# Pooled attention and two feed-forwards on one core: the softmax exponential head by head on ScalarE, straight from PSUM, with its sum from the same instruction

## The chip, the cores and the metric

The kernel runs on one core of a Trainium2 chip. The metric is device time in microseconds (us) of one execution. A core has TensorE (matrix products), VectorE, ScalarE and GpSimd, and SyncE, which here only issues transfers. The profile calls them PE, DVE, ACT, POOL and SP; each takes its instructions in order.

## What is computed

Attention over pooled keys and values, then a feed-forward with a squared relu, then a gated one:

```python
k_p = k.reshape(B, H, Sp, pool, D).mean(axis=3)      # 8 batches, 8 heads, 72 pooled keys, D = 64
v_p = v.reshape(B, H, Sp, pool, D).mean(axis=3)
scores = scale * np.matmul(q, k_p.transpose(0, 1, 3, 2))
scores = scores - np.max(scores, axis=-1, keepdims=True)
attn = np.exp(scores)
attn = attn / (np.sum(attn, axis=-1, keepdims=True) + 1e-09)
x = np.matmul(attn, v_p)                             # 4608 tokens of 512
h = np.maximum(x @ w_in, 0.0)
x = (s * (h * h) + b) @ w_out                        # 2048 wide
out = sigmoid(x @ w_gate) * (x @ w_val) @ w_out2     # 1536 wide
```

The feed-forward weights come as 64-bit words and are converted to float32 on the chip. Every product of the feed-forwards is made of three passes over a high and a low part of its operands.

## The kernel before

The 4608 tokens are cut into 18 **units** of 256 tokens, a unit into two **halves** of 128 (t = 0, 1), and the 8 heads into two groups of four (c = 0, 1). For a half, `scores` makes two score tiles in PSUM (`sps`, 128 tokens x 4 heads x 72 keys), takes the maximum over keys (`mx`), subtracts it into an SBUF tile `e` of 8 x 72 columns, and after the second group takes the exponential of all of `e` in one ScalarE instruction. `norm` sums `e` over keys (`sm`), scales and inverts the sum, and GpSimd multiplies: `pm` holds keys 0 to 63, `pl` the last 8. `left` splits `pl` into `lt`; `turn` transposes `pm` (`tm`) and `lt` (`tl`) on TensorE and splits the results; `values` makes the value product `pv`, whose split is the input `xh`, `xl` of the first feed-forward.

In PSUM the pool `ps_c` has two buffers. Score tiles (from unit 2 on), `tm`, `tl` and `pv` take them in turn: for a half both buffers go to its two score tiles, and the next two tiles of the pool wait until these have been read.

The first feed-forward runs in steps, 16 for each block of 512 tokens: `emit_h` (into `hps`), an evacuation and square on ScalarE and VectorE, a split into `gh` and `gl` (L55, L56), and two steps later `emit_x` (into `acc`). Its weights are converted during the first 16 steps, by ScalarE (L80, L55), VectorE (L81 to L83) and GpSimd (L56). The attention of unit u is strewn over these steps by a table of events: scores of half 0 at the beginning of a span of eight steps, of half 1 two steps later, `turn` of half 0 one step behind those, and so on. The weights of the second feed-forward are prepared beside steps 18 and on (`prep_w2`, again L80 to L83). The second feed-forward begins when all 144 steps are done and has no attention.

What sets the order on the engines: units 0 and 1 stand in an order written by hand. In the first 16 steps a scheduler orders all engines; from step 16 on TensorE's order is that of the code, and the scheduler orders the others. Pool buffers and data give the waits.

Of the kernel before, what the change touches and what calls it, by code (L numbers as in the profile page):

```python
# [8 lines left out]
F32 = mybir.dt.float32  # L9
F32R = mybir.dt.float32r  # L10
I32 = mybir.dt.int32
ACTF = mybir.ActivationFunctionType
ALU = mybir.AluOpType
AX = mybir.AxisListType
# [5 lines left out]
def pooled_attention_two_ffn(ctx, tc, q, k, v, v_left, w_in, w_out, s_in, b_in, w_gate, w_val, w_out2, out):  # L20
# [8 lines left out]
    nc = tc.nc  # L29
    NT, DM = out.shape  # L30
    NU, _, NP, UNIT = q.shape
    B, _, _, POOL, _, SP = k.shape
    S = SP * POOL
    D = 64
    H = 2 * NP
# [64 lines left out]
    at2 = at_stack.enter_context(tc.tile_pool(name="at2", bufs=2, side="right"))  # L100
# [235 lines left out]
    q_t, e_t, l_t, t_t = {}, {}, {}, {}  # L336

    def segs(t0, n):

        done = 0  # L340
        while done < n:
            b, s = divmod(t0 + done, S)
            step = min(n - done, S - s)
            yield done, step, b, s
            done += step
# [8 lines left out]
    s_t = {}  # L354

    def scores(u, t, c, pool=None):
        if c == 0:
            s_t[u, t] = (at2.tile([128, H, SP], F32, tag="e", name="e"), at2.tile([128, H], F32, tag="mx", name="mx"))
        e, mx = s_t[u, t]
        ps = (ps_a if pool else ps_c).tile([128, 4, SP], F32, tag="a" if pool else "c", name="sps")  # L360
        for i in range(2):
            for off, n, b, _ in segs(u * UNIT + t * 128, 128):
                nc.tensor.matmul(
                    out=ps[off:off + n, 2 * i:2 * i + 2, :].rearrange("p h j -> p (h j)"),
                    lhsT=q_t[u][:, 2 * i + c, t * 128 + off:t * 128 + off + n],
                    rhs=kbd[b % 2][:, 2 * i + c].rearrange("p two j -> p (two j)"),
                    start=True, stop=True,
                )
        h = slice(4 * c, 4 * c + 4)
        nc.vector.tensor_reduce(out=mx[:, h], in_=ps, axis=AX.X, op=ALU.max)  # L370
        nc.vector.tensor_tensor(out=e[:, h], in0=ps, in1=mx[:, h].unsqueeze(2).to_broadcast([128, 4, SP]),
                                op=ALU.subtract)
        if c == 1:
            nc.scalar.activation(out=e, in_=e, func=ACTF.Exp, scale=1.0 / (POOL * float(D) ** 0.5))
            if t == 1:
                q_t.pop(u)

    def norm(u, t, early=False):
        e, _ = s_t.pop((u, t))
        sm = at2.tile([128, H], F32, tag="sm", name="sm")  # L380
        nc.vector.tensor_reduce(out=sm, in_=e, axis=AX.X, op=ALU.add)
        nc.vector.tensor_scalar(out=sm, in0=sm, scalar1=float(POOL), scalar2=POOL * 1e-9, op0=ALU.mult, op1=ALU.add)
        nc.vector.reciprocal(out=sm, in_=sm)
        if early:
            pm = gp.tile([128, 512], F32, tag="g", name="pm", bufs=2).rearrange("p (h j) -> p h j", h=H)
        else:
            pm = at1.tile([128, H, 64], F32, tag="pm", name="pm")
        pl = at2.tile([128, H, 8], F32, tag="pl", name="pl")
        for o, j in ((pl, slice(64, SP)), (pm, slice(0, 64))):
            nc.gpsimd.tensor_tensor(out=o, in0=e[:, :, j], in1=sm.unsqueeze(2).to_broadcast(list(o.shape)), op=ALU.mult)  # L390
        e_t[u, t] = pm, pl
# [76 lines left out]
    for u in range(2, NU):  # L468
        p = 16 * (u - 2) + (2 if u == 2 else 0)
        for t, o in ((0, 0), (1, 4)):  # L470
            at(p + o, scores, u, t, 0)
            at(p + o, scores, u, t, 1)
            at(p + o + 2, norm, u, t)
            at(p + o + 3, left, u, t)
            if t == 0:
                at(p + 6, turn, u, 0, 0)
                at(p + 6, turn, u, 0, 1)
        at(p + 10, turn, u, 1, 0)
        at(p + 10, turn, u, 1, 1)
        at(p + 7, load_q, u + 2)  # L480
        at(p + 12, values, u, 0)
        at(p + 13, values, u, 1)

    def probs(u, t):
        scores(u, t, 0, True)
        scores(u, t, 1, True)
# [5 lines left out]
    with tc.manual_schedule():  # L492
# [22 lines left out]
        probs(0, 0)  # L515
        probs(0, 1)
        norm(0, 0, True)
        pool_v_pe(0, "v")
        left(0, 0)
        probs(1, 0)  # L520
        norm(0, 1, True)
        turns(0, 0)
        place_v(0)
# [16 lines left out]
    if True:  # L540
# [61 lines left out]
        for i in range(NS):  # L602
# [7 lines left out]
            x, r = divmod(i - 20, 8)  # L610
# [205 lines left out]
```

## Time and profile before

| | us |
|---|---|
| median of 3 runs | 1792.96 (1792.5 to 1793.54) |
| profiled execution | 1793.74 |
| its span | 1792.0 |
| busy: PE, DVE, ACT, POOL | 1739.8, 937.2, 774.8, 550.1 |

The span is from the first to the last instruction of the profiled execution; the 1.7 us around it are start and end. Busy times are sums over an engine's instructions. The mean granted clock of TensorE is 0.989 of full speed; only the first slices of the page show less than 9 tenths.

### The profile page before, as it was taken

To read this page: it belongs to the slowest core of one execution; us is meant where nothing else is said; L and a number is where in the kernel's file an instruction comes from. 1 tells how busy PE (TensorE), PEld (TensorE's weight loads), DVE (VectorE), ACT (ScalarE), POOL (GpSimd) and SP (SyncE) were. 2 spreads that over 40 slices of the span, in tenths; PEclk is the share of its full clock that TensorE was granted. 3 is DMA by queue.
4 is the path that set the end of the run, shared out by engine and by line. 5 is a ranking of instruction groups with operands and counts; after the bars stand their busy time and mean duration, and the time that the engine had idled before them with its cause. 6 is when DMAs were issued, how large, how long until landed. Compare 5 with 4: busy or idle time off the path is not lost.

```text
span 1792.0 us, 21860 instructions
## 1 busy us (share of the span) xinstructions
PE 1739.8 (97%) x8064; PEld 1446.9 (81%) x8064; DVE 937.2 (52%) x1491; ACT 774.8 (43%) x1390; POOL 550.1 (31%) x592
## 2 busy tenths in 40 slices
PE   5788999999999999999999999999999999999999
PEld 4667888888888888888887888888888888888887
DVE  6897747556465656444443545554545454545111
ACT  2566444444444545444444434343424343444122
POOL 3764504224042322010002443144314431443132
PEclk8989999999999999999999999999999999999999
DMA  6776735647383736332433334733473347333642
GB/s 229 261 227 211 273 123 198 223 165 250 112 267 123 265 118 223 118 118 94 141 106 144 118 109 146 251 114 113 144 253 110 117 141 256 106 118 115 235 140 83
DMA packets 84282, 298.18 MB, mean 166 GB/s; under 512 B 9808, under 2 KB 10832, under 8 KB 84176
## 3 DMA queue, kind: packets, MB, share of 16 engines
q1 hardware_dynamic: 80976, 286.30, 46.7%
q0 software_dynamic: 3200, 10.49, 1.7%
q8 instruction: 64, 1.05, 0.2%
q14 instruction: 42, 0.34, 0.1%
HBM read 250.61 MB, written 46.14 MB: 166 GB/s over the span
## 4 chain that ended last, share of the span: by engine, by line
PE 72%; issue 4%; DMA 1%; POOL 1%; DVE 0%; ACT 0%; POOLq 0%; DVEq 0%
PE pc L664 5%; PE pc L663 5%; PE pc L662 5%; PE acc L718 5%; PE acc L720 5%; PE acc L719 5%; PE pb L664 4%; PE pb L663 4%; PE pb L662 4%; PE hps L196 4%; PE hps L198 4%; PE hps L197 4%; PE acc L227 4%; PE acc L229 4%; PE acc L228 4%
## 5 line engine op out<-in xcount | busy, mean ns | idle before, releaser
L56 POOL TENSOR_TENSOR w<-w 128x512 fp32r<-128x512 f32 x264 | 254.4, 996 | 505.2 <-ACT w L55 481.7
L668 DVE TENSOR_TENSOR wk<-pc,wk 128x512 f32<-128x512 f32 x192 | 132.3, 689 | 240.8 <-PE pc L664 240.7
L196 PE MATMUL hps<-xl,wi 128*128 128x512 f32 (+1 forms) x584 | 234.5, 402 | 5.5 <-ACT g L200 2.6
L198 PE MATMUL hps<-xh,wi 128*128 128x512 f32 (+1 forms) x584 | 227.4, 389 | 0.0
L197 PE MATMUL hps<-xh,wi 128*128 128x512 f32 (+1 forms) x584 | 227.1, 389 | 0.0
L227 PE MATMUL acc<-gl,woh 128*128 128x512 f32 x576 | 225.5, 391 | 0.2 <-DVE gl L56 0.2
L228 PE MATMUL acc<-gh,woh 128*128 128x512 f32 x576 | 225.2, 391 | 0.0
L229 PE MATMUL acc<-gh,wol 128*128 128x512 f32 x576 | 225.0, 391 | 0.0
L56 DVE TENSOR_TENSOR gl<-g,gh 128x512 fp32r<-128x512 f32 x204 | 156.7, 768 | 129.6 <-ACT gh L55 124.6
L55 ACT ACTIVATE gh<-g 128x512 fp32r<-128x512 f32 x204 | 128.2, 628 | 142.5 <-DVE g L680 139.7
L204 DVE TENSOR_TENSOR g<-g 128x512 f32<-128x512 f32 x128 | 97.9, 765 | 150.3 <-ACT g L200 150.3
L205 ACT ACTIVATE g<-g,b_sb,s_sb 128x512 f32<-128x512 f32 x144 | 117.3, 814 | 126.4 <-DVE g L204 125.6
L662 PE MATMUL pc<-xo,w 128*128 128x512 f32 x432 | 168.1, 389 | 0.0
L664 PE MATMUL pc<-xo,w 128*128 128x512 f32 x432 | 168.1, 389 | 0.0
L663 PE MATMUL pc<-xo,w 128*128 128x512 f32 x432 | 168.0, 389 | 0.0
L200 ACT ACTIVATE g<-hps 128x512 f32<-128x512 f32 x144 | 85.3, 593 | 176.5 <-PE hps L198 174.6
L55 ACT ACTIVATE w<-w 128x512 fp32r<-128x512 f32 x264 | 113.3, 503 | 100.4 <-DMA w<-w7d 100.4
L664 PE MATMUL pb<-xo,w 128*128 128x512 f32 x336 | 131.6, 392 | 1.7 <-POOL w L56 1.7
L196 PEld LDWEIGHTS hps<-xl,wi 128*128 128x128 f32 x584 | 111.0, 190 | 26.8 <-ACT g L200 2.8
L662 PE MATMUL pb<-xo,w 128*128 128x512 f32 x336 | 131.3, 391 | 0.5 <-ACT w L55 0.5
L663 PE MATMUL pb<-xo,w 128*128 128x512 f32 x336 | 131.2, 390 | 0.0
L198 PEld LDWEIGHTS hps<-xh,wi 128*128 128x128 f32 x584 | 110.6, 189 | 23.5
(113 smaller groups left out, 3245.5 us busy)
## 6 DMA issues: line engine op xcount, KB each, us to landing
wi<-w1d SPq DMA_DIRECT2D x128, 512.0 KB, 3.4
wo<-wo2d SPq DMA_DIRECT2D x108, 512.0 KB, 3.5
w<-w7d SPq DMA_DIRECT2D x48, 896.0 KB, 4.4
raw<-in SPq DMA_DIRECT2D x68, 512.0 KB, 4.6
kv<-in SPq DMA_DIRECT2D x24, 512.0 KB, 5.2
kv<-in SPq DMA_DIRECT2D x16, 576.0 KB, 4.7
cv<-x2d POOLq DMA_DIRECT2D x36, 256.0 KB, 5.9
out<-eo SPq DMA_DIRECT2D x36, 256.0 KB, 4.2
```

The costliest lines, as they stand in the source:

```text
L55: nc.scalar.activation(out=hi, in_=src, func=ACTF.Copy)
L56: eng.tensor_tensor(out=lo, in0=src, in1=hi.bitcast(F32), op=ALU.subtract)
L196: nc.tensor.matmul(out=ps[:, f], lhsT=hi[:, kk], rhs=c[:, kk, f], start=kk == 0, stop=False)
L197: nc.tensor.matmul(out=ps[:, f], lhsT=hi[:, kk], rhs=a[:, kk, f], start=False, stop=False)
L198: nc.tensor.matmul(out=ps[:, f], lhsT=lo[:, kk], rhs=a[:, kk, f], start=False, stop=kk == KD - 1)
L227: nc.tensor.matmul(out=acc[j][d], lhsT=hi[:, f], rhs=gl, start=m == 0, stop=False)
L228: nc.tensor.matmul(out=acc[j][d], lhsT=hi[:, f], rhs=gh, start=False, stop=False)
L229: nc.tensor.matmul(out=acc[j][d], lhsT=lo[:, f], rhs=gh, start=False, stop=m == M1 - 1)
L662: nc.tensor.matmul(out=ps, lhsT=w[:, 0, x, kk], rhs=r[:, 1, kk, :n], start=first and kk == 0, stop=False, skip_group_check=True)
L663: nc.tensor.matmul(out=ps, lhsT=w[:, 0, x, kk], rhs=r[:, 0, kk, :n], start=False, stop=False, skip_group_check=True)
L664: nc.tensor.matmul(out=ps, lhsT=w[:, 1, x, kk], rhs=r[:, 0, kk, :n], start=False, stop=kk == 1, skip_group_check=True)
L668: nc.vector.tensor_tensor(out=o, in0=ps, in1=b_, op=ALU.add)
```

## The change

The subtraction on VectorE and the sum over keys on VectorE are taken out. VectorE now multiplies the maximum by minus the scale, and ScalarE takes the exponential of each head by itself, from PSUM, with that as its bias, and writes the head's sum over keys with the same instruction (`accum_out`).

```diff
     def scores(u, t, c, pool=None):
         if c == 0:
-            s_t[u, t] = (at2.tile([128, H, SP], F32, tag="e", name="e"), at2.tile([128, H], F32, tag="mx", name="mx"))
-        e, mx = s_t[u, t]
+            s_t[u, t] = (at2.tile([128, H, SP], F32, tag="e", name="e"), at2.tile([128, H], F32, tag="mx", name="mx"),
+                         at2.tile([128, H], F32, tag="sm", name="sm"))
+        e, mx, sm = s_t[u, t]
+        scale = 1.0 / (POOL * float(D) ** 0.5)
...
         nc.vector.tensor_reduce(out=mx[:, h], in_=ps, axis=AX.X, op=ALU.max)
-        nc.vector.tensor_tensor(out=e[:, h], in0=ps, in1=mx[:, h].unsqueeze(2).to_broadcast([128, 4, SP]),
-                                op=ALU.subtract)
-        if c == 1:
-            nc.scalar.activation(out=e, in_=e, func=ACTF.Exp, scale=1.0 / (POOL * float(D) ** 0.5))
-            if t == 1:
-                q_t.pop(u)
+        nc.vector.tensor_scalar(out=mx[:, h], in0=mx[:, h], scalar1=-scale, scalar2=None, op0=ALU.mult)
+        for i in range(4):
+            x = 4 * c + i
+            nc.scalar.activation(out=e[:, x], in_=ps[:, i], func=ACTF.Exp, scale=scale, bias=mx[:, x:x + 1], accum_out=sm[:, x:x + 1])
+        if c == 1 and t == 1:
+            q_t.pop(u)
 
     def norm(u, t, early=False):
-        e, _ = s_t.pop((u, t))
-        sm = at2.tile([128, H], F32, tag="sm", name="sm")
-        nc.vector.tensor_reduce(out=sm, in_=e, axis=AX.X, op=ALU.add)
+        e, _, sm = s_t.pop((u, t))
```

The order on ScalarE at the start of the program, with the engines that an instruction waits for behind it. Before (`e` is the exponential, `t` and `v1h` are splits of transposes and values):

```order
L374 ACT_TABLE_LOAD
L374 ACTIVATE e<-e 128x576 [waits DVE_49] x2
L398 ACTIVATE lt<-pl 128x16x8 [waits Pool_49]
L374 ACTIVATE e<-e 128x576 [waits DVE_49,Activation_49,Pool_49]
L55 ACTIVATE t_274<-tm 128x4x128 [waits PE_49]
```

and of the change:

```order
L376 ACT_TABLE_LOAD [waits DVE_49]
L376 ACTIVATE e,sm<-sps,mx 128x72 [waits PE_49]
L376 ACTIVATE e,sm<-sps,mx 128x72 x3
L376 ACTIVATE e,sm<-sps,mx 128x72 [waits DVE_49,PE_49]
L376 ACTIVATE e,sm<-sps,mx 128x72 x3
L376 ACTIVATE e,sm<-sps,mx 128x72 [waits DVE_49,PE_49]
L376 ACTIVATE e,sm<-sps,mx 128x72 x3
L376 ACTIVATE e,sm<-sps,mx 128x72 [waits DVE_49,PE_49]
L376 ACTIVATE e,sm<-sps,mx 128x72 x3
L398 ACTIVATE lt<-pl 128x16x8 [waits Pool_49]
```

Sixteen short instructions stand where two long ones stood, and the load of ScalarE's function table waits for VectorE, where it waited for nothing. Behind the `lt` of the first half come eight more in place of one, and then the split of `tm`.

On VectorE, in unit 1 (`raw` is a weight tile that is being converted), before:

```order
L370 TENSOR_REDUCE mx<-sps 128x4
L81 TENSOR_SCALAR raw<-raw 128x512
L371 TENSOR_TENSOR e<-sps,mx 128x288
L370 TENSOR_REDUCE mx<-sps 128x4
L371 TENSOR_TENSOR e<-sps,mx 128x288
L381 TENSOR_REDUCE sm<-e 128x8
```

and of the change:

```order
L372 TENSOR_REDUCE mx<-sps 128x4
L81 TENSOR_SCALAR raw<-raw 128x512
L373 TENSOR_SCALAR mx<-mx 128x4
L372 TENSOR_REDUCE mx<-sps 128x4
L373 TENSOR_SCALAR mx<-mx 128x4
L382 TENSOR_SCALAR sm<-sm 128x8
```

A multiply stands in the place of each subtraction, the sum over keys is gone, and L81 has kept its place between the maximum and what uses it.

On VectorE, at the second half of unit 9, where the scheduler sets the order, before:

```order
L399 TENSOR_TENSOR lt<-pl,lt 128x16x8
L56 TENSOR_TENSOR gl<-g,gh 128x512
L204 TENSOR_TENSOR g<-g 128x512
L56 TENSOR_TENSOR gl<-g,gh 128x512
L370 TENSOR_REDUCE mx<-sps 128x4 x2
L371 TENSOR_TENSOR e<-sps,mx 128x288 x2
L381 TENSOR_REDUCE sm<-e 128x8
```

and of the change:

```order
L56 TENSOR_TENSOR gl<-g,gh 128x512
L204 TENSOR_TENSOR g<-g 128x512
L56 TENSOR_TENSOR gl<-g,gh 128x512
L372 TENSOR_REDUCE mx<-sps 128x4 x2
L373 TENSOR_SCALAR mx<-mx 128x4 x2
L382 TENSOR_SCALAR sm<-sm 128x8
```

The two maxima stand behind the same splits as before; behind them two multiplies have taken the place of the two subtractions.

## Rows read from the trace of the kernel before

**Rows 1.** Busy us (instructions) by engine in two stretches, granted clock, DMA share, GB/s.

```profile
core 0: us, PE busy (x) PEld busy (x) DVE busy (x) ACT busy (x) POOL busy (x), PEclk, DMA share, GB/s
45.00:165.00 120.00, 98.59 (x478) 80.69 (x479) 110.97 (x157) 78.12 (x144) 78.70 (x62) 0.93 0.74 248
165.00:850.00 685.00, 682.41 (x3349) 573.14 (x3348) 386.68 (x654) 320.50 (x548) 179.89 (x197) 1.00 0.52 177
```

**Rows 2.** Groups by line and shape: count, busy us, mean ns, idle before.

```profile
L371 DVE TENSOR_TENSOR e<-sps,mx 128x288 f32<-128x288 f32 x72 | 30.4, 446 | 0.3
L381 DVE TENSOR_REDUCE sm<-e 128x8 f32<-128x576 f32 x36 | 26.9, 748 | 15.0 <-ACT e L374 15.0
L374 ACT ACTIVATE e<-e 128x576 f32<-128x576 f32 x36 | 24.6, 684 | 73.6 <-DVE e L371 73.4
L398 ACT ACTIVATE lt<-pl 128x128 fp32r<-128x128 f32 x36 | 10.8, 300 | 16.7 <-POOL pl L390 16.6
L205 ACT ACTIVATE g<-g,b_sb,s_sb 128x512 f32<-128x512 f32 x144 | 117.3, 814 | 126.4 <-DVE g L204 125.6
L55 ACT ACTIVATE wi<-cv 128x512 fp32r<-128x512 f32 x16 | 10.0, 628 | 14.8 <-DVE cv L83 14.8
```

**Rows 3.** Timeline of the start: start us, duration us, engine, line, operation.

```profile
0.74 1.28 ACT L374 ACT_TABLE_LOAD   x1 [0.74 <-PEq L807]
...
8.94 0.46 DVE L370 TENSOR_REDUCE mx<-sps 128x4 f32<-128x288 f32 x1
...
20.03 0.43 DVE L81 TENSOR_SCALAR raw<-raw 128x512 int32<-128x512 int32 x1 [2.75 <-DMA raw<-in]
...
21.80 0.68 ACT L374 ACTIVATE e<-e 128x576 f32<-128x576 f32 x1 [6.71 <-DVE e L371]
22.39 0.58 ACT L55 ACTIVATE t<-tm 128x512 fp32r<-128x512 f32 x1
...
25.90 0.46 DVE L370 TENSOR_REDUCE mx<-sps 128x4 f32<-128x288 f32 x1
...
28.60 0.28 ACT L329 ACTIVATE lh<-vps 128x128 fp32r<-128x128 f32 x1
...
32.43 0.55 PE L433 MATMUL pv<-t,v1h 128*128 128x256 f32 x1 [5.82 <-DVE t L56]
```

**Rows 4.** Instructions on `sm`, 45 to 165 us: shortest, median, longest ns.

```profile
L382 DVE TENSOR_SCALAR sm<-sm x4: 157/465/1301, 77.9 to 149.8; 128x8 f32<-128x8 f32 x4
```

**Rows 5.** What TensorE waited for, 45 to 165 us: us, times, longest.

```profile
PE tl L421 <- DVE e L371: 5.8, 2, 4.6
```

**Rows 6.** Timeline of unit 9, second half.

```profile
444.57 0.81 DVE L370 TENSOR_REDUCE mx<-sps 128x4 f32<-128x288 f32 x2
...
446.53 0.38 PE L421 MATMUL tl<-ident,lt 128*128 128x128 f32 x2
```

**Rows 7.** Timeline of units 7, 11, 13 and 4, second half.

```profile
344.12 0.81 DVE L370 TENSOR_REDUCE mx<-sps 128x4 f32<-128x288 f32 x2
...
346.98 0.38 PE L421 MATMUL tl<-ident,lt 128*128 128x128 f32 x2
...
542.37 0.81 DVE L370 TENSOR_REDUCE mx<-sps 128x4 f32<-128x288 f32 x2
...
544.70 0.38 PE L421 MATMUL tl<-ident,lt 128*128 128x128 f32 x2
...
642.04 0.81 DVE L370 TENSOR_REDUCE mx<-sps 128x4 f32<-128x288 f32 x2
...
644.18 0.38 PE L421 MATMUL tl<-ident,lt 128*128 128x128 f32 x2
...
194.45 0.45 DVE L371 TENSOR_TENSOR e<-sps,mx 128x288 f32<-128x288 f32 x1
...
195.04 0.41 PE L421 MATMUL tl<-ident,lt 128*128 128x128 f32 x2
```

**Rows 8.** Timeline of unit 10, second half.

```profile
492.25 0.45 DVE L371 TENSOR_TENSOR e<-sps,mx 128x288 f32<-128x288 f32 x1
...
495.45 0.38 PE L421 MATMUL tl<-ident,lt 128*128 128x128 f32 x2
```

## The prediction

> **What bounds the kernel now.** I read the busy times by stretch first. From 165 to 850 us TensorE is busy 682.41 of 685 us, at full granted clock, while VectorE is busy 387 and ScalarE 320 [rows 1]. There an instruction of VectorE or ScalarE costs nothing in itself; it costs when a matmul has to wait for it. From 45 to 165 us it is otherwise: VectorE is busy 111 of 120 us, TensorE 99, ScalarE 78, because the weights of the first feed-forward are converted there beside the attention [rows 1]. Before 45 us units 0 and 1 run as one chain over all engines: TensorE's first value product starts at 32.43 us after an idle time of 5.82 us on VectorE [rows 3]. So the change is weighed in three places: A, the start; B, the stretch up to 165 us; C, the stretch behind it, where only a wait of TensorE counts.
>
> **What goes.** 72 subtractions at 446 ns and 36 sums over keys at 748 ns leave VectorE (59 us in all), and 36 exponentials of 576 columns at 684 ns leave ScalarE (24.6 us) [rows 2]. **What comes.** 72 small multiplies on VectorE, and 288 exponentials of 72 columns on ScalarE.
>
> The price of one such exponential, called h (start to start), decides most. Columns cost (684 - 300) / (576 - 128) = 0.86 ns, so a ScalarE instruction of 72 columns takes 300 - 56 x 0.86 = 252 ns [rows 2]. It has a bias in memory: the line with scale and bias from memory takes 814 ns where a plain one of the same shape takes 628, 93 ns for each such operand [rows 2]. That makes 345 ns, and instructions in a row overlap by 0.09 us (the exponential of 21.80 us ends at 22.48, the next starts at 22.39 [rows 3]): h = 0.25 us if the sum comes for nothing. The trace has no ScalarE instruction that writes a sum. If the sum has to be read out by a second instruction as short as the shortest here (0.30 us), without overlap, h = 0.64. I take 0.45, the middle: the sum is there only when the last column has passed, so I expect it to cost something, but not that nothing overlaps.
>
> On this the Trainium skill (ScalarE: Activation LUTs, What ACT_TABLE_LOAD costs) says that an ACTIVATE with a bias pointer takes about 280 ns plus 0.833 ns a column, with about 93 ns of overlap. An estimate from this page is 340 ns and h = 0.25, as the rows give; it names no price for the accumulator output, so by the page alone the sum below would be +2.7 us.
>
> A multiply has no row either; the nearest is the VectorE TENSOR_SCALAR on 128x8 of L382: 157 ns at its shortest, 1301 at its longest, 0.6 on average between 45 and 165 us (four of them: 157, two around 465, 1301 [rows 4]). GpSimd runs then, and these small SBUF operations vary while the sum on the same tile does not. I take 0.17 outside B and 0.6 in B, with 0.16 and 1.30 as ends.
>
> **A, the start.** The order here is written by hand and stays. VectorE waits for raw weights until 20.03 us in any case, with L81 between maximum and subtraction of unit 1 [rows 3]; that hides the load of ScalarE's table, which the new program lets wait for the first multiply (8.94 + 0.46 + 0.17 us, then 1.28 us with the gaps: 10.95), and the first 16 exponentials: 10.95 + 16 x 0.45 = 18.2 us. At h = 0.64 they end at 21.2 and, with the residue split behind them, 2.6 us stick out. Then eight exponentials run from 20.75 (L81's end, 20.46, and a multiply) to 20.75 + 8h; behind them on ScalarE stands the split that now starts at 22.39: later by 8h - 1.6 us. In the same way the maxima of 25.90 let exponentials start at 26.65 and the lh copy, which starts at 28.60 now, is later by 8h - 1.95 [rows 3]. It leads through VectorE to the value product at 32.43. One sum over keys (0.74 us) that stands ahead of the weight conversion is gone. Together 16h - 4.3 us: +2.9 at 0.45, -0.3 and +5.9 (+8.5 with what sticks out) at the ends.
>
> **B, 45 to 165 us.** Four halves of a unit: VectorE is relieved of 8 x 0.446 + 4 x 0.748 = 6.5 us and loaded with 8 x 0.6 = 4.8 us; as it is the busiest engine I count the difference in full, -1.7 us (ends: -5.2 and +3.9). Against it, two waits of TensorE there, 5.8 us, end with a subtraction that frees a PSUM buffer [rows 5]. Now four exponentials free it, later by 4h - 0.44 each: 8h - 0.9. B is 8h - 2.6: +1.0 us.
>
> **C, from 165 us.** Both buffers of `ps_c` are taken by the two score tiles of a half, and the next to want them are the transposes `tm` and `tl` of the first half, one step behind the scores of the second. Now VectorE alone frees them, 0.8 us after the two maxima. Afterwards eight exponentials must run first. In unit 9 the maxima start at 444.57, both multiplies are done by 445.65, so `tl`, which starts at 446.53 today [rows 6], would start at 445.65 + 8 x 0.45 = 449.25: 8h - 0.9 = 2.7 us of idle TensorE, at full price, since nothing behind it in TensorE's order may pass. The maxima are that late because VectorE has in front of them a split that waits for ScalarE, and the new order leaves that split in front of them. Units 7, 11 and 13 read alike, with 8h - 1.8, 8h - 1.25 and 8h - 1.1; in unit 4 only the second tile is late (its subtraction starts at 194.45, `tl` at 195.04): 4h - 0.4 [rows 7]. In the other units the maxima come early: in unit 10 the last subtraction starts at 492.25 and `tl` at 495.45, 1.2 us of room behind four exponentials [rows 8]. I take the nine units of this kind as free. C is 36h - 5.4: +10.8 us, +3.6 and +17.6 at the ends.
>
> **The sum.** A + B + C = 60h - 12.3 = +14.7 us at h = 0.45. The profiled execution took 1793.74 us with a span of 1792.0, 0.8 above the median of 1792.96; on the median the forecast is 1807.7 us.
>
> **Rivals.**
> *The sum is free*, h = 0.25: 60 x 0.25 - 12.3 = +2.7, 1795.7 us. For it: the rows price the instruction itself no higher. Against it: nothing shows what a sum costs.
> *The exponentials count, the PSUM wait does not*: the late maxima hang on splits that wait for ScalarE, and those on raw weights from DMA; if these arrive differently in the new order, the maxima come early as in unit 10, and A + B is left: +3.9, 1796.9 us. Against it: the lateness repeats in every second unit from 7 to 13.
> *Two instructions per head*, h = 0.64: 60 x 0.64 - 12.3 + 2.6 = +28.7, 1821.7 us. Eight then hold ScalarE for 5.1 us, in which the evacuation of `hps` stands behind them too. The Trainium skill (VectorE: DVE Perf Modes, Two Vector instructions with no wait between them) says that on VectorE an operation that also writes out its accumulator is two instructions; for ScalarE no run here shows it.
> *Faster*: VectorE is the bound of B and nothing else. With multiplies at 0.16 us B gives 8 x 0.25 - 0.9 - 5.2 = -4.1, A -0.3, and with early maxima C is nothing: -4.4, 1788.6 us. It needs h under about 0.25 and no late unit; with the late units of today it is lost again from h = 0.14 on, where 36h - 5.4 passes zero.
>
> **Chances.** Forecast 0.58; free sum 0.14; no PSUM wait 0.13; two instructions 0.08; faster 0.07. A change of 0.2% (3.6 us) is about what a measurement of this kernel can tell from none. The free sum falls within it mostly, the case without the PSUM wait half: same 0.18, slower 0.75, faster 0.07. The range runs from the free sum less part of the cheap multiplies, 1794, to two instructions, 1822; the forecast's own is 1800 to 1816 (h from 0.33 to 0.58).
>
> **What would show it.** The new profile should have ScalarE near 775 - 25 + 288 x 0.45 = 880 us busy, VectorE about 40 us less (59 less 72 multiplies of 0.17 to 0.6). TensorE's waits behind 165 us should be led by `tl` and `tm` waiting for ScalarE's exponentials, some 11 us in four or five units, 2 to 3 us each, and nothing else of size. In the start the lh copy should run near 31.5 us and the first value product near 35. Wrong it would be if the sum has another price than 0.45, if the maxima of the late units move, or if VectorE's relief moves the end of the conversions by more than 2 us.

## The result, and the profile after

The changed kernel took 1803.41 us (median of 8 runs, 1795.74 to 1806.51); the kernel before, on the same chip, 1792.2. The ratio is 1.0052, 95% interval 1.0039 to 1.0066: slower by some 9 us, where the forecast was 14.7. The two medians lie 11.2 us apart; the ratio counts fast runs alone, which leaves out one run of the kernel before that took 4526.51 us. The profiled execution took 1804.39 us, its span 1802.6.

The page's busy times, after:

```profile
PE 1746.9 (97%) x8064; PEld 1450.2 (80%) x8064; DVE 894.5 (50%) x1455; ACT 840.3 (47%) x1930; POOL 552.9 (31%) x592
```

VectorE has 42.7 us less, ScalarE 65.5 more. TensorE has as many matmuls as before, but is busy 7.1 us longer: some ran at a lower clock. Groups by line, to be read beside [rows 2]:

```profile
L376 ACT ACTIVATE e<-sps,mx 128x72 f32<-128x72 f32 x288 | 87.8, 328 | 55.0 <-DVE mx L373 54.7
L376 ACT ACTIVATION_READ_ACCUMULATOR e<-sps,mx 128x1 f32 x288 | 61.7, 214 | 0.0
L373 DVE TENSOR_SCALAR mx<-mx 128x4 f32<-128x4 f32 x72 | 15.9, 236 | 0.3
```

The sum is a second instruction of its own, 214 ns on average. The timeline shows how much of it counts (first two and last of eight heads in unit 1; weight conversion and the next two steps of the start, as in [rows 3]):

```profile
18.60 0.43 DVE L81 TENSOR_SCALAR raw<-raw 128x512 int32<-128x512 int32 x1 [1.62 <-DMA raw<-in]
19.22 0.32 ACT L376 ACTIVATE e<-sps,mx 128x72 f32<-128x72 f32 x1 [3.21 <-DVE mx L373]
19.44 0.19 ACT L376 ACTIVATION_READ_ACCUMULATOR e<-sps,mx 128x1 f32 x1
19.53 0.31 ACT L376 ACTIVATE e<-sps,mx 128x72 f32<-128x72 f32 x1
...
21.30 0.35 ACT L376 ACTIVATE e<-sps,mx 128x72 f32<-128x72 f32 x1
...
27.66 0.32 ACT L329 ACTIVATE lh<-vps 128x128 fp32r<-128x128 f32 x1
...
31.02 0.55 PE L433 MATMUL pv<-t,v1h 128*128 128x256 f32 x1 [5.80 <-DVE sm L382]
```

The eighth head starts 21.30 - 19.22 = 2.08 us behind the first: h is 2.08 / 7 = 0.297 us (the expectations below say 0.295), since the next exponential starts while the sum is read. The start is not later than before. Both stretches, beside [rows 1]:

```profile
45.00:165.00 120.00, 104.22 (x500) 84.88 (x501) 105.69 (x154) 85.58 (x205) 74.96 (x62) 0.92 0.73 251
165.00:850.00 685.00, 672.88 (x3271) 563.00 (x3270) 350.90 (x614) 362.34 (x939) 182.18 (x193) 0.99 0.51 174
```

Up to 165 us TensorE does more than before (104.22 us of work against 98.59); behind it, it idles 12 us where it idled 2.6. What it waited for from 165 to 900 us:

```profile
PE pv L433 <- DVE t L56: 5.5, 3, 2.7
PE tm L415 <- ACT e L376: 3.9, 1, 3.9
PE tl L421 <- ACT e L376: 1.9, 3, 0.8
PE tm L415 <- issue: 0.9, 1, 0.9
```

Taken by where TensorE stands in its order, the scores of unit 4, second half, start at 183.88 us after and 188.08 before: 4.2 us gained. Those of unit 17, second half, start at 848.51 and 836.76. The stretches between the two, before and after (columns as in [rows 1]):

```profile
188.08:836.76 648.68, 646.09 (x3173) 542.56 (x3172) 369.77 (x623) 303.64 (x520) 169.50 (x184) 1.00 0.52 179
183.88:848.51 664.63, 652.51 (x3173) 545.85 (x3172) 341.87 (x597) 352.11 (x910) 174.56 (x184) 0.99 0.51 175
```

The same 3173 matmuls take 16 us more. TensorE idles 12.1 us in place of 2.6, and its work takes 6.4 us longer. So A and B are a gain and C is a loss of more than the whole difference.

### The profile page after: what moved, and what is told of

Its sections match the earlier page's. It is cut to its first block, busy times and chain, and to the rows that moved or that the text cites. A ratio compares the mean times of both kernels' runs of the same rounds, so it can differ in the third digit from the quotient of the medians.

```text
span 1802.6 us, 22435 instructions
## 1 busy us (share of the span) xinstructions
PE 1746.9 (97%) x8064; PEld 1450.2 (80%) x8064; DVE 894.5 (50%) x1455; ACT 840.3 (47%) x1930; POOL 552.9 (31%) x592
## 4 chain that ended last, share of the span: by engine, by line
PE 76%; issue 5%; DMA 4%; DVE 3%; ACT 2%; POOL 1%; SPq 0%; DVEq 0%; POOLq 0%; ACTq 0%
PE pc L664 5%; PE pc L663 5%; PE pc L662 5%; PE acc L718 5%; PE acc L720 5%; PE acc L719 5%; PE hps L196 5%; PE hps L198 5%; PE hps L197 5%; PE acc L227 5%; PE acc L229 5%; PE acc L228 5%; PE pb L664 4%; PE pb L663 4%; PE pb L662 4%
## 5 line engine op out<-in xcount | busy, mean ns | idle before, releaser
L55 ACT ACTIVATE gh<-g 128x512 fp32r<-128x512 f32 x204 | 128.5, 630 | 143.6 <-DVE g L680 140.5
L55 ACT ACTIVATE w<-w 128x512 fp32r<-128x512 f32 x264 | 113.3, 503 | 100.8 <-DMA w<-w7d 100.8
L390 POOL TENSOR_TENSOR pl<-e,sm 128x64 f32<-128x64 f32 x36 | 22.4, 622 | 371.8 <-ACT g L200 336.0
L227 PEld LDWEIGHTS acc<-gl,woh 128*128 128x128 f32 x576 | 108.7, 189 | 31.4 <-DVE gl L56 9.6
L664 PE MATMUL pb<-xo,w 128*128 128x512 f32 x336 | 130.8, 389 | 1.7 <-POOL w L56 1.7
```

The costliest lines, as they stand in the source:

```text
L55: nc.scalar.activation(out=hi, in_=src, func=ACTF.Copy)
L227: nc.tensor.matmul(out=acc[j][d], lhsT=hi[:, f], rhs=gl, start=m == 0, stop=False)
L664: nc.tensor.matmul(out=ps, lhsT=w[:, 1, x, kk], rhs=r[:, 0, kk, :n], start=False, stop=kk == 1, skip_group_check=True)
```

## The experiments

Intervals are 95%, ratios against the kernel before in the same series of runs; differences in us against it are taken from these ratios, and against another kernel from the two times. "The new form" is the changed softmax, "the old form" that of before.

**The new form in some units only.**

```diff
         nc.vector.tensor_reduce(out=mx[:, h], in_=ps, axis=AX.X, op=ALU.max)
...
+        if u < 4:
+            nc.vector.tensor_scalar(out=mx[:, h], in0=mx[:, h], scalar1=-scale, scalar2=None, op0=ALU.mult)
...
+        else:
+            nc.vector.tensor_tensor(out=e[:, h], in0=ps, in1=mx[:, h].unsqueeze(2).to_broadcast([128, 4, SP]),
+                                    op=ALU.subtract)
+            if c == 1:
+                nc.scalar.activation(out=e, in_=e, func=ACTF.Exp, scale=scale)
...
+        if not (u < 4):
+            nc.vector.tensor_reduce(out=sm, in_=e, axis=AX.X, op=ALU.add)
```

The condition is `u < 4` in e_early and e_early2, `u >= 4` in e_late, `u < 2` in e_start and `u in (2, 3)` in e_mid.

Units 0 to 3 new (e_early): 

> The new form (exponential per head from PSUM, sum with it) is used for units 0 to 3 only, the old form for units 4 to 17. Theory: the change gains about 4 us up to 165 us (TensorE reached unit 5 about 3 us earlier in the changed kernel than before) and loses 13 to 16 us behind it, so this kernel should be 3 to 5 us faster than before, 1788 to 1790 us, with no wait of TensorE on exponentials behind 170 us. Rival 1, the terms of the forecast with the measured price of 0.295 us a head (A + B = 24 x 0.295 - 6.9 = +0.2): 1792 to 1793. Rival 2, the loss behind 165 us comes from the changed phase in which the start leaves the program, not from the form of the softmax there: then part of the loss shows here too, 1795 or more.

It took 1788.28 us, ratio 0.9972 (0.9961 to 0.9982). Waits of TensorE, 165 to 900 us:

```profile
PE tm L423 <- POOL pm L398: 3.5, 3, 2.2
```

Once more (e_early2): 

> The new form for units 0 to 3, the old behind, once more, unaltered, beside its two halves: 1788.3 us the first time (0.28% faster than before). If that holds, 1787 to 1790 and an interval below 1; if it was the chance of one series, 1791 to 1794.

1788.39 us, 0.9968 (0.9956 to 0.998). The change gains 5 to 6 us where VectorE is the busiest engine, and this version beats both kernels.

Units 4 to 17 new (e_late): 

> The reverse: the old form for units 0 to 3, the new one for units 4 to 17. Theory: all of the loss is here, 13 to 16 us against before, 1805 to 1808 us, slower than the changed kernel, with waits of tm and tl on exponentials in units 4 to 13. Rival 1, the forecast's term C alone at 0.295 us a head (36 x 0.295 - 5.4 = +5.2): 1797 to 1798. Rival 2, the loss hangs on the phase set by the start: 1792 to 1796.

1802.4 us, 1.0052 (1.004 to 1.0064): a loss of 9.3 us, between the theory and the first rival. Waits, 165 to 900 us:

```profile
PE pv L441 <- DVE t L56: 4.3, 2, 2.7
PE tm L423 <- ACT e L377: 3.9, 1, 3.9
PE tl L429 <- ACT e L377: 1.9, 3, 0.8
```

They are the waits of the changed kernel, so the loss doesn't hang on the start. But the parts don't add up: -5 and +9 make +4, and both together are +9; why stays open. From the scores of unit 4 on, the profile of this kernel loses 12 us, that of the changed one 16.

Units 0 and 1 alone (e_start): 

> The new form for units 0 and 1 alone (the start, term A of the forecast), the old one behind. The forecast's A with the measured price of a head is 16 x 0.295 - 4.3 = +0.4 us; in the changed kernel TensorE reached unit 2 0.5 us earlier than before. Both say: within 1 us of before, 1792 to 1795. Rival: the gain up to 165 us comes from the start (the weight conversions begin earlier, as one sum over keys no longer stands ahead of them): then 3 to 5 us faster, 1788 to 1790.

1792.18 us, 0.9983 (0.9973 to 0.9993): 3.1 us faster by the ratio, which is the rival's gain, but 2.1 us by the medians (the kernel before took 1794.27 in this series), between the rival and my two numbers. Units 2 and 3 alone (e_mid): 

> The new form for units 2 and 3 alone (45 to 165 us, term B of the forecast). Theory: VectorE is the busiest engine there and its relief counts in full, about -3.5 us, 1789 to 1791. The forecast's B with the measured price of a head is 8 x 0.295 - 2.6 = -0.2 us: 1792.5 to 1794. Rival: the gain needs both parts together: within 1 us of before as well, while the kernel with both parts stays at 1788.

1792.58 us, 0.9991 (0.9982 to 1.0): -1.6 us, half of what the theory said, with an interval that reaches to no change. By the ratios the two halves, -3.1 and -1.6, about make up what both gave together; by the medians, -2.1 and -1.7 of -5.9, they don't.

**Who frees the PSUM buffer.** In e_sub VectorE subtracts into `e` as before; the exponentials stay eight a half:

```diff
-        nc.vector.tensor_scalar(out=mx[:, h], in0=mx[:, h], scalar1=-scale, scalar2=None, op0=ALU.mult)
+        nc.vector.tensor_tensor(out=e[:, h], in0=ps, in1=mx[:, h].unsqueeze(2).to_broadcast([128, 4, SP]),
+                                op=ALU.subtract)
...
-            nc.scalar.activation(out=e[:, x], in_=ps[:, i], func=ACTF.Exp, scale=scale, bias=mx[:, x:x + 1], accum_out=sm[:, x:x + 1])
+            nc.scalar.activation(out=e[:, x], in_=e[:, x], func=ACTF.Exp, scale=scale, accum_out=sm[:, x:x + 1])
```

> All units: VectorE subtracts the maximum into e as before (and so frees the PSUM buffer), ScalarE takes the exponential head by head from e, with the sum from the same instruction. ScalarE has the same number of instructions as in the changed kernel; only who frees the PSUM buffers differs. Theory, PSUM hold: the waits of tm and tl on exponentials are gone behind 165 us, and the time is within 4 us of before, 1790 to 1796 (VectorE saves the 36 sums, 27 us). Rival, ScalarE's longer chain itself delays what follows (hps evacuation, t splits): 1800 or more, with TensorE's waits led by pv and hps instead.

1796.16 us, 1.0016 (1.0005 to 1.0027). Waits, 165 to 900 us:

```profile
PE pv L434 <- DVE t L56: 1.4, 1, 1.4
PE tm L416 <- DVE e L373: 0.8, 1, 0.8
PE pv L434 <- ACT g L200: 0.7, 1, 0.7
```

No wait on exponentials is left, and from unit 4 on this profile takes 650.9 us (before 648.7): as many instructions on ScalarE, but C is nearly gone. The waits of `pv` are shorter too. The gain ahead of it is gone too: the scores of unit 4, second half, start at 188.08, as before, though VectorE is rid of the sums.

**The same waits with room.** In e_turn8 `tm` and `tl` of the first half stand one step later in TensorE's order:

```diff
-                at(p + 6, turn, u, 0, 0)
-                at(p + 6, turn, u, 0, 1)
+                at(p + (8 if u >= 4 else 6), turn, u, 0, 0)
+                at(p + (8 if u >= 4 else 6), turn, u, 0, 1)
```

> The changed kernel with one thing moved: from unit 4 on the transposes tm and tl of half 0 stand one step (some 5 us of matmuls) later in TensorE's order, behind the scores of half 1 with room for eight exponentials. Theory, PSUM buffers held by the exponentials: the waits of tm and tl on exponentials (5.8 us behind 165 us in the changed kernel) are gone, and with them the lower clock that follows each; the gain up to 165 us (4 us) is then left over, so 1789 to 1796, depending on the waits of pv for the t split (5.5 us), which this does not take away and may lengthen. Rival, ScalarE's load or the order on VectorE delays everything behind the scores alike: tm waits no longer but pv and hps wait as much more, 1800 to 1806.

1792.39 us, 0.9988 (0.9979 to 0.9997): 10.4 us less than the changed kernel in the same series (1802.74, e_again below), of which it is a copy but for this. From the scores of unit 4 to those of unit 17 it takes 651.0 us. Waits, 165 to 900 us, and the stretch:

```profile
PE tl L421 <- DVE t L56: 1.2, 3, 0.5
PE pv L433 <- DVE t L56: 1.2, 2, 0.8
PE tm L415 <- POOL pm L390: 1.0, 2, 0.8
```

```profile
165.00:850.00 685.00, 681.44 (x3333) 570.56 (x3333) 348.28 (x625) 372.70 (x965) 189.20 (x196) 1.00 0.51 175
```

ScalarE is busier than in the changed kernel (372.70 us against 362.34, since more of the program falls into the stretch), and behind 165 us nothing waits for its exponentials. `pv` waits less, not more, which I had not expected.

The same move with the old form behind unit 3 (e_early8): 

> The new form for units 0 to 3 only, the old one behind, and tm and tl of half 0 one step later from unit 4 on. The kernel with the new form for units 0 to 3 took 1788.3 us and had left only three waits of tm for GpSimd's pm behind 165 us (3.5 us, with lower clock after them about 2.8 us of lost time against the matmuls). Theory: the step more hides these, 1784 to 1787. Rival: the later split of tm pushes the t split before pv: pv waits 1 to 2 us in several units, 1788 to 1795.

1793.02 us, 0.9996 (0.9987 to 1.0005). The theory failed, and the rival had the time right but not the cause: `pv` doesn't wait, and the wait for GpSimd became longer.

```profile
PE tm L423 <- POOL pm L398: 6.1, 3, 2.6
```

A likely reason, argued and not tried: `pm` has one buffer, which `tm` of the first half must have read before GpSimd may write the second half's. GpSimd's timeline in unit 6 shows what stands between `pl` and `pm` now; without the move `pm` followed `pl` at once (298.89 and 299.60 us, and `tm` at 301.14). In this unit `tm` of the first half is done by 297.9, so the buffer is free when `pl` runs: what holds `pm` up here is its place in GpSimd's order. All of what the move does can explain only about half of the 4 to 5 us between the two kernels: from unit 4 on the profile is 2.5 us longer, and it is 2.2 us behind already there, where both are the same code.

```profile
300.79 0.75 POOL L398 TENSOR_TENSOR pl<-e,sm 128x64 f32<-128x64 f32 x1
301.50 1.74 POOL L269 TENSOR_TENSOR kv<-kv 128x512 f32<-128x512 f32 x1
303.19 1.17 POOL L175 TENSOR_TENSOR raw<-raw,cv 128x256 f32<-128x256 f32 x1
304.33 1.09 POOL L398 TENSOR_TENSOR pm<-e,sm 128x512 f32<-128x512 f32 x1
```

**The exponentials twice over (e_double).**

```diff
-        for i in range(4):
+        for i in 2 * list(range(4)) if u >= 4 else range(4):
```

> The changed kernel with the suspected cost doubled: from unit 4 on each half takes its eight exponentials twice over (sixteen instructions, the second pass writes the same values). Theory, PSUM buffers held while the exponentials run: in the units that wait now the wait is longer by 8 x 0.295 = 2.4 us, and units 7, 9 and others join, so by the forecast's slope of 36 heads some 10 us, with lower clock after each wait up to 16: 1812 to 1820, and tm and tl on exponentials lead TensorE's waits with 15 us or more. Rival, the loss comes from where VectorE's maxima and t splits stand, not from the time of the exponentials: less than 4 us more than the changed kernel, 1803 to 1807.

1836.68 us, 1.0233 (1.0219 to 1.0246). More than either said: 33 us over the changed kernel. Waits, 165 to 900 us:

```profile
PE tl L421 <- ACT e L376: 14.3, 13, 2.2
PE tm L415 <- issue: 11.1, 4, 3.6
```

`tl` waits for exponentials 13 times in place of 3. The direction is the theory's; the slope of 36 heads, which counts five units, is far too flat once the others have used up their room.

**What the sum costs (e_nosum).** No `accum_out`, and VectorE sums as before:

```diff
-            nc.scalar.activation(out=e[:, x], in_=ps[:, i], func=ACTF.Exp, scale=scale, bias=mx[:, x:x + 1], accum_out=sm[:, x:x + 1])
+            nc.scalar.activation(out=e[:, x], in_=ps[:, i], func=ACTF.Exp, scale=scale, bias=mx[:, x:x + 1])
...
+        nc.vector.tensor_reduce(out=sm, in_=e, axis=AX.X, op=ALU.add)
```

> As the changed kernel, but without the sum in the exponential: eight exponentials a half from PSUM with the bias, the sum over keys by VectorE as before. It prices the sum. If reading the accumulator costs time on ScalarE, the pitch of the heads falls from 0.295 to about 0.24 us (328 ns less 0.09 of overlap) and the waits of tm and tl on exponentials shrink by a sixth; the 36 sums (27 us) return to VectorE, so 1800 to 1804 us in all. If the read is hidden under the next exponential, the pitch stays at 0.295 and the kernel is as slow as the changed one or slower, 1803 to 1808.

1796.12 us, 1.0014 (1.0003 to 1.0026), 7 us under the changed kernel and below both expectations. Timeline, unit 11, second half:

```profile
541.29 1.80 ACT L376 ACTIVATE e<-sps,mx 128x72 f32<-128x72 f32 x8 [2.30 <-DVE mx L373]
```

Eight heads take 1.80 us, where with sums they take some 2.5. At the group's mean of 334 ns, 8 x 0.334 - 1.80 = 0.87 us overlap in seven places, 0.125 each, so h is 0.209 without the sum: the sum costs 0.09 us a head. The profiled run, 1791.54 us, is one of the shortest of 12 (1790.91 to 1801.62); what the longer ones waited for isn't seen.

**One exponential for four heads (e_shared)**, with one maximum for the four (another number is subtracted; the softmax is the same):

```diff
-        nc.vector.tensor_reduce(out=mx[:, h], in_=ps, axis=AX.X, op=ALU.max)
-        nc.vector.tensor_scalar(out=mx[:, h], in0=mx[:, h], scalar1=-scale, scalar2=None, op0=ALU.mult)
-        for i in range(4):
...
+        m = mx[:, 4 * c:4 * c + 1]
+        nc.vector.tensor_reduce(out=m, in_=ps.rearrange("p h j -> p (h j)"), axis=AX.X, op=ALU.max)
+        nc.vector.tensor_scalar(out=m, in0=m, scalar1=-scale, scalar2=None, op0=ALU.mult)
+        nc.scalar.activation(out=e[:, h], in_=ps, func=ACTF.Exp, scale=scale, bias=m)
...
+        nc.vector.tensor_reduce(out=sm, in_=e, axis=AX.X, op=ALU.add)
```

> All units: one maximum for four heads of a token in place of one for each (softmax is unchanged by which number is subtracted), so that a single exponential of 288 columns from PSUM, with that as its bias, does what four did; the sum over keys is VectorE's again. ScalarE then needs about 0.53 us a group (300 + 160 x 0.86 ns + 0.09), two a half, 1.0 us against 2.4. Theory, the price of eight short exponentials between maximum and release is what costs: the release comes 1.4 us earlier than in the changed kernel, nearly as early as before, so almost no waits behind 165 us, and the subtraction's relief of VectorE remains: 1788 to 1792. Rival, ScalarE's place between maximum and release costs in itself (its queue holds evacuations that wait): waits of tm and tl stay above 3 us, 1797 or more.

1795.85 us, 1.0009 (0.9999 to 1.0019): between the two. Waits, 165 to 900 us:

```profile
PE pv L433 <- DVE t L56: 3.3, 2, 2.4
PE tm L415 <- ACT e L375: 0.3, 1, 0.3
```

The wait on exponentials is 0.3 us: their place in ScalarE's queue costs little in itself. The waits of `pv` are left, though ScalarE takes two exponentials a half in place of eight. The profiled run (1790.9) is the shortest of 11, which reach to 1798.14; what holds the others up stays open.

**The changed kernel again (e_again).** 

> The changed kernel once more, unaltered, for a second profile and more times: its first runs lay at 1796 (two) and at 1802 to 1806 (six). Theory: the late waits behind 165 us depend on how the weight conversion beside them happens to fall; the static order is the same, but where raw weights land some 3 us later against the scores (unit 11 of the first profile), the maxima, eight exponentials and tm follow late. Then a profile of a run near 1796 lacks the 3.9 us wait of tm in unit 11 (idle and lower clock together about 6 us), and one near 1803 has it again. Rival: the waits are fixed by the order, and the levels differ somewhere else (start or second feed-forward): then unit 11 shows 3 to 4 us of wait in either case.

1802.74 us, 1.0042 (1.0027 to 1.0056); the profiled run took 1804.38. Waits, 165 to 900 us:

```profile
...
PE tm L415 <- ACT e L376: 3.2, 1, 3.2
PE tl L421 <- ACT e L376: 2.6, 3, 1.5
```

The large wait came back in the same unit. That a run near 1796 lacks it wasn't seen, since neither of the two profiles fell on one.

## Why the prediction was right, and where its steps were not

The time lies in the forecast's own range (1800 to 1816), and the mechanism that carries its largest term is one that the runs show, though it is not all of the loss. That the number fits is in part luck: at the measured price of a head the forecast's own sum is 60 x 0.297 - 12.3 = +5.5 us, 1798.5 us, below its range, whose h went from 0.33 to 0.58. A and B were forecast 9 us too high, and C lacked two costs, which cancels in part. Two of the forecast's own signs of being wrong came true: the sum has another price, and the maxima of units 7, 9 and 11 moved.

**h**, the price of a head, was taken as 0.45 and is 0.297. The instruction itself was priced well (345 ns worked out, 328 found), and the sum is a second instruction, as in the rival of two instructions; but most of it lies under the next exponential, so it adds 0.09 us, where 0.20 was taken (0.45 less 0.25) and 0.39 feared. ScalarE's busy time is 840 us in place of 880 for that; VectorE's 43 us less were forecast as 40. An estimate from the Trainium skill (ScalarE: Activation LUTs, What ACT_TABLE_LOAD costs), 280 ns plus 0.833 ns a column, is 340 ns for such an ACTIVATE; the traces agree (328 with the sum, 334 without). What the Trainium skill says of VectorE (VectorE: DVE Perf Modes, Two Vector instructions with no wait between them), that writing out an accumulator is an instruction of its own, is what this trace shows of ScalarE (288 rows of each), but without the second one's length counting in full.

**A and B** were +2.9 and +1.0 and are a gain. With h = 0.297 their formulas give together +0.2; timed, units 0 and 1 give -3.1 us, units 2 and 3 -1.6, both -5.0 and -5.7. In A I looked at the path to the first value product only. It starts at 31.02 us in place of 35, and before at 32.43 [rows 3]; the 1.4 us is what the raw weights landed earlier in this execution (L81 at 18.60, before 20.03). Other profiles say the same: with either form the product starts 12.4 us behind L81 (e_early2, new form: 20.07 and 32.48; e_late, old form: 19.50 and 31.91). So the exponentials cost nothing there, and what e_start gains is gained behind it. The likely source, not tried by itself: VectorE is rid of 8 subtractions and 4 sums there (6.6 us by [rows 2]) for 8 multiplies, and behind the start it is the busiest engine. I had counted one of these sums. In B I counted two PSUM waits as longer [rows 5]; of the waits of 45 to 165 us these are now the longest and the only one on exponentials:

```profile
PE acc L227 <- DVE gl L56: 8.0, 3, 4.6
...
PE sps L365 <- ACT e L376: 1.5, 2, 0.8
```

Those were 5.8 us for `tl` on a subtraction; TensorE now gets past them and waits for `gl` instead; in all it works 5.6 us more in the stretch. Eight multiplies cost VectorE 3.8 us there, 4.8 were taken. Which part of the relief helps can be read from all the profiles: in the nine profiles without a subtraction up to unit 4 its second half's scores start between 181.4 and 184.9 us (two of these kernels, e_nosum and e_shared, have the sums on VectorE), in the two with it in part of the units at 185.2 (e_mid) and 186.1 (e_start), in the three with it in all at 186.0 (e_late), 188.1 (before) and 188.1 (e_sub, without the sums). So it seems to be the subtraction. One execution differs from another by 2 us here, as before and e_late show, so that the times of e_early carry the size, not these.

**C** was +10.8. Measured alone (e_late) it is +9.3; taken as what is left of the changed kernel's loss when the gain of e_early is set against it, +13 to +14 (9.3 + 5.0; 7.5 + 5.7 with e_again and e_early2). The mechanism holds: take away what makes `tm` and `tl` wait, by who reads the PSUM tile (e_sub) or by room in TensorE's order (e_turn8), and C is nearly gone, with ScalarE as loaded as ever. But both kernels also shorten the waits of `pv` (5.5 us to 2.1 and 1.2), so that they don't divide the loss between the two. And the sum over units came out near only by chance: `tm` and `tl` wait 6.7 us in three units, not 11 in five, and at the measured h the formula gives 5.3. Unit 4 was 4h - 0.4 = 0.8 us, unit 13 8h - 1.1 = 1.3 at the measured h. TensorE's timeline in units 4, 11 and 13 [rows 7]:

```profile
191.93 0.44 PE L421 MATMUL tl<-ident,lt 128*128 128x128 f32 x2 [0.82 <-ACT e L376]
...
550.79 0.63 PE L415 MATMUL tm<-ident,pm 128*128 128x128 f32 x4 [3.86 <-ACT e L376]
551.95 0.53 PE L421 MATMUL tl<-ident,lt 128*128 128x128 f32 x2 [0.54 <-ACT e L376]
...
654.44 0.63 PE L415 MATMUL tm<-ident,pm 128*128 128x128 f32 x4 [0.90 <-issue]
655.60 0.44 PE L421 MATMUL tl<-ident,lt 128*128 128x128 f32 x2 [0.54 <-ACT e L376]
```

0.82 and 0.90 + 0.54 = 1.44: as worked out. Units 7 and 9 wait not at all, since their maxima came early (unit 9: 443.03, 5.5 us ahead of `tm`; before, 444.57 [rows 6]). Unit 11 waits 4.4 where 8h - 1.25 = 1.1 was due. VectorE's and ScalarE's timeline there:

```profile
547.07 1.12 DVE L56 TENSOR_TENSOR gl<-g,gh 128x512 fp32r<-128x512 f32 x1 [1.54 <-ACT gh L55]
548.11 0.81 DVE L372 TENSOR_REDUCE mx<-sps 128x4 f32<-128x288 f32 x2
...
550.47 0.21 ACT L376 ACTIVATION_READ_ACCUMULATOR e<-sps,mx 128x1 f32 x1
...
551.65 0.24 ACT L376 ACTIVATION_READ_ACCUMULATOR e<-sps,mx 128x1 f32 x1
```

The fourth head is done at 550.68 and `tm` starts at 550.79; the eighth at 551.89, and `tl` starts at 551.95. The maxima stand behind the same `gl` as before, but 7.8 us behind their scores (540.30), where it was 4.6 (537.79 and 542.37 [rows 7]). Some 9 us earlier VectorE stood before a weight tile until 531.14 (before 525.49), 3.1 us later against TensorE; its transfer was issued at 527.27 (before 521.39). Why the conversion of the second feed-forward's weights runs later there was not tried. What I took as a property of the unit, how late its maxima are, is one of the phase between TensorE and the weight conversion, and that has moved. The gain ahead of it alone doesn't set it: e_late, with the old form up to unit 4, has the same wait of 3.9 us in unit 11, and e_nosum, with the new one, has 0.7 for `tm` and `tl` together.

Two things were missing from C. `pv` waited 5.5 us for the split of `tm` in three units, which I named nowhere ("nothing else of size" was wrong); e_turn8 leaves 1.2 of it. This is not a wait for a PSUM buffer. ScalarE and TensorE in unit 6, whose second `tm` starts at 303.06 without a wait:

```profile
305.02 0.63 ACT L55 ACTIVATE raw<-cv 128x512 fp32r<-128x512 f32 x1 [4.60 <-DVE cv L83]
...
309.54 0.58 ACT L55 ACTIVATE t<-tm 128x512 fp32r<-128x512 f32 x1
...
312.03 0.33 PE L433 MATMUL pv<-t,v1h 128*128 128x192 f32 x1 [2.70 <-DVE t L56]
```

ScalarE stands 4.60 us before a weight conversion that waits for VectorE, and the split of `tm` comes behind it; before, the same L55 waited 0.30 us (at 306.52). In unit 8 it waits 5.16, and in e_shared, unit 6, 3.84 with 2.4 for `pv`: so the number of exponentials does not decide it. e_early, with the old form there, has 0.30 and no wait of `pv`. Why the order of the new form makes this wait was not tried.

And a wait costs more than its time. Granted clock (third number from the right) in steps of 1 and 2 us around the wait of unit 11:

```profile
551.00:552.00 1.00, 0.47 (x5) 0.23 (x3) 0.07 (x1) 1.00 (x8) 0.00 (x0) 1.00 0.98 328
...
554.00:555.00 1.00, 1.00 (x4) 0.81 (x3) 0.44 (x2) 1.00 (x3) 1.00 (x2) 0.50 0.09 29
555.00:556.00 1.00, 1.00 (x5) 0.81 (x4) 1.00 (x2) 0.45 (x2) 1.00 (x2) 0.71 0.06 16
556.00:558.00 2.00, 2.00 (x11) 1.65 (x10) 0.95 (x2) 0.60 (x1) 1.01 (x1) 1.00 0.22 35
```

After the idle time the clock is at its lower level, 1.2 GHz, until about 555.3. Matmuls then start 0.43 us apart, not 0.23. From the scores of unit 11, second half, to those of unit 12 TensorE needs 45.1 us, before 38.7: 6.4 more for 4.4 of idle time. So of the 16 us by which the profile is longer from unit 4 on, the waits of `tm` and `tl` are 6.7 and those of `pv` 5.5, in place of 2.6 for `pm` before; the other 6.4 are the same matmuls, slower.

**The rivals.** *The sum is free* was nearer with its price (0.25; measured 0.297) than the forecast, not with its time. *Two instructions* was right in form, not in price. *The exponentials count, the PSUM wait does not* was right for units 7 and 9, whose maxima came early; units 4, 11 and 13 and e_turn8 speak against it. *Faster* was right that VectorE is the bound of B, and its -4.4 us is near what e_early gives, but it put nearly all of that into B, where e_mid has -1.6; it needed C to be nothing, and that takes another kernel. Its sum is off by a little: 36h - 5.4 passes zero at 0.15, not 0.14.

## What to carry to other kernels

An operation moved to an idle engine can still lengthen the time for which a PSUM buffer is held; ask when the reader that frees it is done, and what stands next in TensorE's order for that buffer. Where one stretch is bound by VectorE and the next by TensorE, use the form that each stretch wants: the new form in the first four units and the old one behind them is 0.3% faster than the kernel before, in two series. Where a buffer must be held longer, one step of room in the static order can pay for it (1802.7 to 1792.4 us). Where nothing is held longer the same step can cost (1788.3 to 1793.0 us); see what it delays.

## What was not expected of the hardware

ScalarE's sum output is an instruction of its own (214 ns on average) that overlaps with the next exponential, so that a head of 72 columns costs 0.297 us with the sum and 0.209 without; from SBUF without a bias it is 0.25 with the sum (e_sub, starts at 178.27, 178.53, 178.78 and 179.02 us). And 3.9 us of idle time of TensorE were followed by some 3 us at 1.2 GHz, so that 4.4 us of waiting made the stretch 6.4 us longer.
